# One-token attention over a KV cache: units of eight heads, V as the moving operand, q made transposed, wo loaded last

## The chip, the cores and the metric

The kernel runs on one core of one Trainium2 chip. The metric is the device time of one execution in microseconds (us); lower is better. The engines of the core are named as in the profile: PE is TensorE (PEld its weight loads), DVE is VectorE, ACT is ScalarE, POOL is GpSimd, SP is SyncE, which issues nearly all transfers (DMA) from HBM. Each engine works through its own instructions in program order and waits on semaphores for the others.

## The reference

Four sequences each decode one token. All arrays are bf16.

```python
B, Sq, D = 4, 1, 640;  H, Sk, Dh = 32, 4096, 128;  F = 1728
def _A_ref(x, k_cache, v_cache, wq, wo):
    q = (x @ wq).reshape(B, Sq, H, Dh).transpose(0, 2, 1, 3)
    scores = einsum("bhqd,bhkd->bhqk", q, k_cache) * (Dh ** -0.5)
    p = softmax(scores)
    o = einsum("bhqk,bhkd->bhqd", p, v_cache)
    return o.transpose(0, 2, 1, 3).reshape(B, Sq, H * Dh) @ wo
def _B_ref(x, w1, b1, w2):
    h = einsum("bsd,df->bsf", x, w1) + b1
    sp = log1p(exp(-abs(h))) + where(h > 0, h, 0)
    return einsum("bsf,fd->bsd", h * tanh(sp), w2)
h  = x + _A_ref(layernorm(x), k_cache, v_cache, wq, wo)
h2 = h + _B_ref(layernorm(h), w1, b1, w2)
```

K and V caches are 134 MB each and every element is used once; there is one query for each head and sequence.

## The kernel before

The schedule is manual: the order of the Python statements is the order of the instructions on each engine, and of the transfers on SP's queue. Tiles come from pools; a tile whose buffer is still in use makes its first writer wait, and where that writer is a transfer, everything behind it on SP's queue waits too.

The work is cut into 32 units g of four heads of one sequence. A K unit (L85, L89) is 4 MB: each head's 4096 positions are spread over 32 partitions, so that a partition holds R = 128 positions of 128 numbers, 32 KB. K and V have a pool of two buffers each; wq and later wo share a third (`wbig`).

For each unit, `mul_and_sum` (L288) multiplies K by q in place on DVE (L297), where q has been spread to all partitions (`qbs`), and sums over the 128 numbers of a position on PE: the identity is the stationary operand, K's columns move past it in eights of 64 positions (L304), and DVE adds the last eight (L316). A unit has two parts (`NP`) of two halves (`NQ`), so four multiplies, each followed by eight matmuls of 512 columns. `softmax` (L323) takes the maximum over a partition (L327), turns it into a row on PE (L329), takes the maximum for each head (L334), sends it back to all partitions (L342), and ACT makes the exps (L347) into `e2`, one instruction for each head on its 32 partitions, with the row sum on the side. `pv` (L225) multiplies by V with V as the stationary operand: 128 positions' rows of V are loaded as weights and a 128x4 piece of `e2` moves (L231), 128 times for a unit. After four units `row_sums` and `normalise` give `otn`, and `project` (L274) adds the heads' product with wo into `yT`.

The loop (L357) is a hand-made pipeline. The softmax of unit g-1 is a generator whose steps are put between the multiplies of unit g; after the multiplies of g come the load of K(g+2), pv(g-1), a projection, the load of V(g+1) and, in the first units, the next chunk of q (`q_chunk`, `q_broadcast`, L186 and L200). wo comes in four pieces at units 8 to 11, w1 and w2 at the end in K's freed buffer. Behind the loop are the last softmax, pv and projection, and then the dense part from `hT` (L440) to the output (L557).

Of the kernel before, what the change touches and what calls it, by code (L numbers as in the profile page):

```python
# [16 lines left out]
def kernel(  # L17
# [13 lines left out]

# [7 lines left out]
    G = 4  # L46
    PH = 128 // G
    R = Sk // PH
    NP = 2
    RP = R // NP  # L50
    W = 512 // RP
    HQ = H // G
    NG = HQ * N
    SCALE = float(Dh) ** -0.5
    EPS = 1e-5
    QC = 512
    WOC = 8
    NQ = 2
    DQ = Dh // NQ
    KBUFS = 2  # L60
    VBUFS = 2
    NE2 = 2

    CI = 4
# [7 lines left out]

    consts = ctx.enter_context(tc.tile_pool(name="consts", bufs=1))
    wbig = ctx.enter_context(tc.tile_pool(name="wbig", bufs=1))
    work = ctx.enter_context(tc.tile_pool(name="work", bufs=2))
    kpool = ctx.enter_context(tc.tile_pool(name="kpool", bufs=KBUFS))
    vpool = ctx.enter_context(tc.tile_pool(name="vpool", bufs=VBUFS))

    x_rows = A_x.rearrange("b s d -> (b s) d")
    out_rows = out.rearrange("b s (c p) -> (b s c) p", p=128)  # L80


    def load_kv(pool, tag, cache, g):
        hq, b = divmod(g, N)
        t = pool.tile([128, R, Dh], BF16, tag=tag, name=f"{tag}{g}")  # L85
        view = cache[b, G * hq : G * (hq + 1)].rearrange("h (p r) d -> (h p) r d", p=PH)

        np_ = NP if g == NG - 1 else 1
        for i in range(np_):  # L89
            r0, r1 = i * R // np_, (i + 1) * R // np_  # L90
            nc.sync.dma_start(out=t[:, r0:r1, :], in_=view[:, r0:r1, :])  # L91
        return t

    def load_k(g):
        return load_kv(kpool, "kt", A_k_cache, g)

    def load_v(g):
        return load_kv(vpool, "vt", A_v_cache, g)

    x_bf = consts.tile([N, D], BF16)  # L100
    nc.scalar.dma_start(out=x_bf[:, :], in_=x_rows[:, :])

    wq_sb = wbig.tile([128, DC, H * Dh], BF16, tag="w")
    nc.sync.dma_start(out=wq_sb[:, :, :], in_=A_wq.rearrange("(p c) n -> p c n", c=DC))
    kts, vts = {}, {}
    kts[0] = load_k(0)
    kts[1] = load_k(1)
    vts[0] = load_v(0)
# [8 lines left out]
    mean_f = consts.tile([128, 128], FP32)  # L117
    nc.gpsimd.memset(mean_f[:, :], 1.0 / D)
# [4 lines left out]
    sel = consts.tile([N, N, G, 128], BF16)  # L123
    nc.vector.memset(sel[:, :, :, :], 0.0)
    e2 = [consts.tile([128, R, G], BF16, name=f"e2_{i}") for i in range(NE2)]
    for t in e2:
        nc.gpsimd.memset(t[:, :, :], 0.0)
    rs2 = consts.tile([128, NG, G], FP32)
    nc.gpsimd.memset(rs2[:, :, :], 0.0)
    b1T = consts.tile([128, FC], FP32)  # L130
    nc.gpsimd.memset(b1T[:, :], 0.0)
    otn = consts.tile([128, HQ, N, G], BF16)

    for q in range(G):
        nc.vector.tensor_copy(
            out=sel[:, :, q, q * PH : (q + 1) * PH],
            in_=ident[0:N, 0:N].unsqueeze(2).to_broadcast([N, N, PH]),
        )

    def layernorm_rows(in_sb, out_bf, pool):  # L140
# [3 lines left out]
        for s in range(n_sub):  # L144
# [10 lines left out]
            out=out_bf[:, :],  # L155
            in0=in_sb[:, :],
# [6 lines left out]

# [3 lines left out]
    ln1_bf = consts.tile([N, D], BF16)  # L167
    layernorm_rows(x_bf, ln1_bf, work)
    xT = consts.tile([128, DC, N], BF16)
    xT_res = consts.tile([128, DC, N], FP32)  # L170
    ln1_v = ln1_bf[:, :].rearrange("n (p c) -> n c p", c=DC)
    x_v = x_bf[:, :].rearrange("n (c p) -> n c p", c=DC)
# [8 lines left out]
    q_all = consts.tile([N, H * Dh], BF16)  # L181

    def q_chunk(n):
        q_ps = ps.tile([N, QC], FP32, tag="qq")
        for c in range(DC):
            nc.tensor.matmul(  # L186
                q_ps[:, :],
                lhsT=xT[:, c, :],
                rhs=wq_sb[:, c, n * QC : (n + 1) * QC],
                start=(c == 0),  # L190
                stop=(c == DC - 1),
            )
        nc.scalar.copy(out=q_all[:, n * QC : (n + 1) * QC], in_=q_ps[:, :])  # L193

    def q_broadcast(hq):
        qb_ps = ps.tile([128, N * Dh], FP32, tag="qq")
        for b in range(N):
            for q in range(G):
                h = G * hq + q
                nc.tensor.matmul(  # L200
                    qb_ps[:, b * Dh : (b + 1) * Dh],
                    lhsT=sel[:, b, q, :],
                    rhs=q_all[:, h * Dh : (h + 1) * Dh],
                    start=(q == 0),
                    stop=(q == G - 1),
                )
        nc.scalar.copy(
            out=qbs[:, hq, :, :], in_=qb_ps[:, :].rearrange("p (b d) -> p b d", d=Dh)
        )

    qbs = consts.tile([128, HQ, N, Dh], BF16)

    Q_AT = {-1: (0,), **{g: (g + 1,) for g in range(HQ - 1)}}
    WO_AT = {HQ + i: i for i in range(H // WOC)}
    B1_AT = HQ + len(WO_AT) + 1

    PROJ_AT = {B1_AT + 1 + hq: hq for hq in range(4)}
    PROJ_AT.update({4 * (hq + 1) + 2: hq for hq in range(4, HQ - 1)})
    for hq in Q_AT[-1]:
        q_chunk(hq)  # L220
        q_broadcast(hq)

    ot = {}

    def pv(g):  # L225
        hq, b = divmod(g, N)
        vt = vts.pop(g)
        if b == 0:
            ot[hq] = ps.tile([128, N, G], FP32, tag="ot", bufs=2, name=f"ot{hq}")
        for r in range(R):  # L230
            nc.tensor.matmul(  # L231
                ot[hq][:, b, :],
                lhsT=vt[:, r, :],
                rhs=e2[g % NE2][:, r, :],
                start=(r == 0),
                stop=(r == R - 1),
            )

    rls = {}

    def row_sums(hq):
        l_ps = ps.tile([128, N, G], FP32, tag="small")
        nc.tensor.matmul(  # L243
            l_ps[:, :, :],
            lhsT=ones_f[:, :],
            rhs=rs2[:, hq * N : (hq + 1) * N, :],
            start=True,
            stop=True,
        )
        rls[hq] = work.tile([128, N, G], FP32, tag="rl", name=f"rl{hq}")  # L250
        nc.vector.reciprocal(out=rls[hq][:, :, :], in_=l_ps[:, :, :])  # L251

    def normalise(hq):
        nc.vector.tensor_tensor(
            out=otn[:, hq, :, :],
            in0=ot.pop(hq)[:, :, :],
            in1=rls.pop(hq)[:, :, :],
            op=ALU.mult,
        )

    b1_row = consts.tile([1, F], BF16)

    def f_chunk(rows, c):

        if c < CK * CI:
            k, i = divmod(c, CI)
            block = rows[:, k * 128 * CI : (k + 1) * 128 * CI]
            return block.rearrange("p (i f) -> p i f", i=CI)[:, i, :], 128
        return rows[:, c * 128 : min(F, (c + 1) * 128)], min(F - c * 128, 128)

    yT = ps.tile([128, DC, N], FP32, tag="yT")
    wo_sb = []

    def project(hq):  # L274

        for h in range(hq * G, (hq + 1) * G):
            for c in range(DC):
                nc.tensor.matmul(  # L278
                    yT[:, c, :],
                    lhsT=wo_sb[0][:, h, c * 128 : (c + 1) * 128],  # L280
                    rhs=otn[:, hq, :, h % G],
                    start=(h == 0 and c == 0),
                    stop=(h == H - 1 and c == DC - 1),
                )

    s_of, s_sbs = {}, {}

    def mul_and_sum(g, part):  # L288

        hq, b = divmod(g, N)  # L290
        r0 = part * RP
        kt = kts[g][:, r0 : r0 + RP, :]
        s_ps = ps.tile([128, RP, W], FP32, tag="s", bufs=2, name=f"s{g}_{part}")
        s_of[g, part] = s_ps
        for k in range(NQ):
            d0 = k * DQ
            nc.vector.tensor_tensor(  # L297
                out=kt[:, :, d0 : d0 + DQ],
                in0=kt[:, :, d0 : d0 + DQ],
                in1=qbs[:, hq, b, d0 : d0 + DQ].unsqueeze(1).to_broadcast([128, RP, DQ]),  # L300
                op=ALU.mult,
            )
            for d in range(d0, d0 + DQ, W):
                nc.tensor.matmul(  # L304
                    s_ps[:, :, :],
                    lhsT=ident[:, :],
                    rhs=kt[:, :, d : d + W],
                    start=(d == 0),
                    stop=(d == Dh - W),
                )  # L310
            yield

    def finish_sum(g, part):
        if part == 0:
            s_sbs[g] = work.tile([128, R], FP32, tag="s_sb", name=f"s_sb{g}")
        nc.vector.tensor_reduce(  # L316
            out=s_sbs[g][:, part * RP : (part + 1) * RP],
            in_=s_of.pop((g, part))[:, :, :],
            axis=AX.X,
            op=ALU.add,  # L320
        )

    def softmax(g):  # L323

        s_sb = s_sbs.pop(g)
        pm = work.tile([128, 1], FP32, tag="pm", name=f"pm{g}")
        nc.vector.tensor_reduce(out=pm[:, :], in_=s_sb[:, :], axis=AX.X, op=ALU.max)  # L327
        tr_ps = ps.tile([128, 128 + G], FP32, tag="tr", name=f"tr{g}")
# [99 lines left out]
    for _ in softmax(NG - 1):  # L428
        pass
# [159 lines left out]
```

## Time and profile before

| | |
|---|---|
| median of 3 runs | 678.37 us (678.27 to 678.69) |
| profiled execution | listed by its span: 676.7 us |
| moved by transfers | 284.15 MB, mean 420 GB/s |
| PE busy, PEld busy | 468.9 us (69%), 258.3 us (38%) |
| DVE busy | 353.1 us (52%) |
| ACT busy | 95.0 us (14%) |
| mean granted TensorE clock | 0.768 of full speed |

The span runs from the first to the last instruction; the rest of an execution's time lies around it. Busy times of different engines overlap, so they are not shares of one sum. A group line of the profile gives line, engine, operation, operands, count, busy time, mean nanoseconds of one, and behind the second bar the idle time of the engine just before and what ended most of it. PE's matmuls are pipelined: the duration of one is longer than the distance from one to the next.

### The profile page before, as it was taken

What the parts mean: (1) busy time and instruction counts of PE and PEld (TensorE: products, weight loads), DVE (VectorE), ACT (ScalarE), POOL (GpSimd) and SP (SyncE); (2) the same over time, 40 slices, a digit from 0 to 9 for tenths busy, and PEclk for the clock granted to TensorE, in tenths of its full rate; (3) what the DMA queues carried; (4) which work ended last, traced back from release to release, by engine and by line L of the source; (5) the groups of instructions that cost most, each with busy time, mean ns of one, the idle gap of its engine ahead of it and who ended that gap; (6) DMA issues with size and microseconds to landing.
All of it is one profiled execution on the core that took longest, in us unless ns stands there. A gap on an engine that the chain in (4) does not pass through costs nothing.

```text
span 676.7 us, 12413 instructions
## 1 busy us (share of the span) xinstructions
PE 468.9 (69%) x5761; PEld 258.3 (38%) x5761; DVE 353.1 (52%) x304; ACT 95.0 (14%) x313; POOL 2.4 (0%) x13
## 2 busy tenths in 40 slices
PE   1588988897676585476667767766766776666964
PEld 0234545444343341343334434333433433333444
DVE  2476555456654356336655545665554566555732
ACT  0022012112100111011100111110111111101131
POOL 1000000000000000000000000000000000000000
PEclk9997677887676786688667888766778877667875
DMA  9999999999999999999999999999999999999994
GB/s 378 434 429 431 433 430 430 432 431 432 426 427 422 429 415 411 431 422 431 427 427 426 431 431 431 431 433 431 430 429 429 427 433 429 433 430 425 431 394 165
DMA packets 16364, 284.15 MB, mean 420 GB/s; under 512 B 1268, under 2 KB 7096, under 8 KB 7737
## 3 DMA queue, kind: packets, MB, share of 16 engines
q1 hardware_dynamic: 16304, 283.36, 98.4%
q8 instruction: 45, 0.74, 0.4%
q14 instruction: 7, 0.05, 0.0%
q10 hardware_dynamic: 8, 0.01, 0.0%
HBM read 283.35 MB, written 0.01 MB: 419 GB/s over the span
## 4 chain that ended last, share of the span: by engine, by line
DMA 65%; PE 19%; DVE 14%; issue 1%; SPq 0%; ACT 0%; DVEq 0%
DMA kt<-in_A_k_cache_dram 61%; PE s L304 17%; DVE kt L297 12%; DMA w<-in_B_w_dram 4%; DVE s_sb L316 2%; PE tr L329 1%; PE ot L231 0%; PE h_ps L471 0%; PE y2T L533 0%; PE tr L342 0%; DVE mx L334 0%; SPq L91 0%; DVE tb L516 0%; ACT nbs L344 0%; PE var_ps L448 0%
## 5 line engine op out<-in xcount | busy, mean ns | idle before, releaser
L304 PE MATMUL s<-kt,ident 128*128 128x512 bf16 x1024 | 301.1, 448 | 171.9 <-DVE kt L297 171.5
L297 DVE TENSOR_TENSOR kt<-kt,qbs 128x4096 bf16<-128x4096 bf16 x128 | 291.5, 2279 | 217.9 <-DMA kt<-in_A_k_cache_dram 217.9
L304 PEld LDWEIGHTS <-ident 128*128 128x128 bf16 x1024 | 108.1, 109 | 324.7 <-issue 178.0
L231 PEld LDWEIGHTS <-vt 128*128 128x128 bf16 x4096 | 108.9, 96 | 11.3 <-DMA vt<-in_A_v_cache_dram 2.2
L231 PE MATMUL ot<-e,vt 128*128 128x4 bf16 x4096 | 108.9, 165 | 4.0 <-DMA vt<-in_A_v_cache_dram 2.1
L347 ACT ACTIVATE e<-s_sb,nbs 32x128 bf16<-32x128 f32 x128 | 74.0, 578 | 2.5
L344 ACT COPY nbs<-tr 128x4 f32<-128x4 f32 x32 | 5.2, 162 | 466.4 <-PE tr L342 466.4
L316 DVE TENSOR_REDUCE s_sb<-s 128x64 f32<-128x512 f32 x64 | 43.6, 681 | 4.4 <-PE s L304 4.2
L347 ACT ACTIVATION_READ_ACCUMULATOR e<-s_sb,nbs 32x1 f32 x128 | 32.2, 252 | 0.0
L251 DVE RECIPROCAL rl<-l_ps 128x16 f32<-128x16 f32 x8 | 2.1, 258 | 45.1 <-PE l_ps L243 45.1
L334 DVE TENSOR_REDUCE mx<-tr 1x4 f32<-1x128 f32 x32 | 8.9, 279 | 30.8 <-PE tr L329 30.8
L186 PE MATMUL q_ps<-wq_sb,xT 128*4 128x512 bf16 x40 | 15.0, 525 | 9.2 <-DMA wq_sb<-in_A_wq_dram 9.2
L200 PE MATMUL qb_ps<-q_all,sel 4*128 4x128 bf16 x128 | 14.1, 292 | 5.3 <-ACT q_all L193 5.3
L329 PE MATMUL tr<-ident_f,pm 128*1 128x128 f32 x64 | 16.3, 350 | 1.2 <-DVE pm L327 1.2
L200 PEld LDWEIGHTS <-sel 4*128 4x128 bf16 x128 | 12.8, 131 | 10.9 <-issue 10.9
L193 ACT CAST q_all<-q_ps 4x512 bf16<-4x512 f32 x8 | 4.6, 574 | 75.2 <-PE q_ps L186 75.2
L342 PEld LDWEIGHTS tr<-mx,nscale 1*128 1x128 f32 x64 | 9.4, 183 | 13.8 <-issue 11.4
L329 PEld LDWEIGHTS tr<-ident_f,pm 128*1 128x1 f32 x64 | 2.8, 81 | 26.0 <-issue 26.0
L342 PE MATMUL tr<-mx,nscale 1*128 1x4 f32 x64 | 12.2, 258 | 0.4 <-DVE mx L334 0.4
L327 DVE TENSOR_REDUCE pm<-s_sb 128x1 f32<-128x128 f32 x32 | 9.1, 286 | 1.1
L186 PEld LDWEIGHTS <-xT 128*4 128x4 bf16 x40 | 3.4, 98 | 15.1 <-issue 13.5
L278 PE MATMUL yT<-otn,wo_sb 128*128 128x4 bf16 x160 | 5.6, 166 | 2.8 <-issue 2.5
(74 smaller groups left out, 50.0 us busy)
## 6 DMA issues: line engine op xcount, KB each, us to landing
kt<-in_A_k_cache_dram SPq DMA_DIRECT2D x31, 4096.0 KB, 25.6
vt<-in_A_v_cache_dram SPq DMA_DIRECT2D x31, 4096.0 KB, 32.0
wq_sb<-in_A_wq_dram SPq DMA_DIRECT2D x1, 5120.0 KB, 14.8
wo_sb<-in_A_wo_dram SPq DMA_DIRECT2D x4, 1280.0 KB, 30.6
kt<-in_A_k_cache_dram SPq DMA_DIRECT2D x2, 2048.0 KB, 23.1
vt<-in_A_v_cache_dram SPq DMA_DIRECT2D x2, 2048.0 KB
w<-in_B_w_dram SPq DMA_DIRECT2D x1, 2160.0 KB, 27.8
w<-in_B_w_dram SPq DMA_DIRECT2D x3, 640.0 KB, 19.9
```

What stands on the lines that cost most here:

```text
L186: nc.tensor.matmul(q_ps[:, :], lhsT=xT[:, c, :], rhs=wq_sb[:, c, n * QC : (n + 1) * QC], start=(c == 0), stop=(c == DC - 1),)
L200: nc.tensor.matmul(qb_ps[:, b * Dh : (b + 1) * Dh], lhsT=sel[:, b, q, :], rhs=q_all[:, h * Dh : (h + 1) * Dh], start=(q == 0), stop=(q == ...
L231: nc.tensor.matmul(ot[hq][:, b, :], lhsT=vt[:, r, :], rhs=e2[g % NE2][:, r, :], start=(r == 0), stop=(r == R - 1),)
L278: nc.tensor.matmul(yT[:, c, :], lhsT=wo_sb[0][:, h, c * 128 : (c + 1) * 128], rhs=otn[:, hq, :, h % G], start=(h == 0 and c == 0), stop=(h ...
L297: nc.vector.tensor_tensor(out=kt[:, :, d0 : d0 + DQ], in0=kt[:, :, d0 : d0 + DQ], in1=qbs[:, hq, b, d0 : d0 + DQ].unsqueeze(1).to_broadcas ...
L304: nc.tensor.matmul(s_ps[:, :, :], lhsT=ident[:, :], rhs=kt[:, :, d : d + W], start=(d == 0), stop=(d == Dh - W),)
L316: nc.vector.tensor_reduce(out=s_sbs[g][:, part * RP : (part + 1) * RP], in_=s_of.pop((g, part))[:, :, :], axis=AX.X, op=ALU.add,)
L327: nc.vector.tensor_reduce(out=pm[:, :], in_=s_sb[:, :], axis=AX.X, op=ALU.max)
L329: nc.tensor.matmul(tr_ps[0:1, 0:128], lhsT=pm[:, :], rhs=ident_f[:, :], start=True, stop=True)
L334: nc.vector.tensor_reduce(out=mx[:, :], in_=tr_ps[0:1, 0:128].rearrange("o (a b) -> o a b", a=G), axis=AX.X, op=ALU.max,)
L342: nc.tensor.matmul(nb_ps, lhsT=nscale[:, :], rhs=mx[:, :], start=True, stop=True)
L347: nc.scalar.activation(out=e2[g % NE2][p0:p1, :, q], in_=s_sb[p0:p1, :], func=ACT.Exp, bias=nb[p0:p1, q : q + 1], scale=SCALE, accum_out=r ...
```

## The change

A unit u is now eight heads of one sequence (`G = 8`, 16 units), and a K or V unit is 64 KB to a partition (R = 256 positions on each of 16 partitions a head), 8 MB in one transfer. K, V, and the weights take turns in three slots of one pool: first wq (with x, its layernorm and b1 behind it in the same slot), then K(0), K(1), V(0), K(2), V(1), and so on, at the end wo with w1, and w2 with the small tiles of the dense part. The exps use all 128 partitions at a time: for head i the bias is the head's maximum on its own 16 partitions and -1e30 elsewhere (`own`), so that other heads' rows come out as zero. V is the moving operand: 32 columns of `e2` (eight heads by four positions) are the stationary one, and 512 columns of V move past them, 64 times a unit; the wanted diagonal of the 32 x 512 result is picked out by four fp32 matmuls with `sel`. q is made transposed, all heads at the start, wq as the stationary operand, and is spread to the partitions for each unit by an ACT copy (`qx`), a matmul with the identity and another ACT copy. The softmax is no longer cut into steps that stand between the multiplies of the next unit. wo is laid out with eight rows to a partition and is loaded behind the last V; the attention output is regrouped to that layout (`regroup`) and projected only behind the last unit. b1 is transposed at the start.

```diff
-    G = 4
+    G = 8
 ...
-    NP = 2
-    RP = R // NP
+    NO = H // G
+    NU = NO * N
+    RP = 64
+    NP = R // RP
 ...
+    slots = ctx.enter_context(tc.tile_pool(name="slots", bufs=3))
     consts = ctx.enter_context(tc.tile_pool(name="consts", bufs=1))
-    wbig = ctx.enter_context(tc.tile_pool(name="wbig", bufs=1))
     work = ctx.enter_context(tc.tile_pool(name="work", bufs=2))
-    kpool = ctx.enter_context(tc.tile_pool(name="kpool", bufs=KBUFS))
-    vpool = ctx.enter_context(tc.tile_pool(name="vpool", bufs=VBUFS))
+    one = ctx.enter_context(tc.tile_pool(name="one", bufs=1))
 ...
+    qT_ps = ps.tile([128, H, N], FP32, tag="qq", name="qT_ps")
+    for h in range(H):
+        for c in range(DC):
+            nc.tensor.matmul(
+                qT_ps[:, h, :],
+                lhsT=wq_sb[:, c, h * Dh : (h + 1) * Dh],
+                rhs=xT[:, c, :],
 ...
+    def q_broadcast(u):
+        o, b = divmod(u, N)
+        qx = one.tile([128, G, PH], BF16, tag="qx", name=f"qx{u}")
+        nc.scalar.copy(
+            out=qx[:, :, :],
+            in_=qT[:, G * o : G * (o + 1), b].unsqueeze(2).to_broadcast([128, G, PH]),
+        )
+        qb_ps = ps.tile([128, Dh], FP32, tag="qq", name=f"qb_ps{u}")
+        nc.tensor.matmul(
+            qb_ps[:, :],
+            lhsT=qx[:, :, :],
+            rhs=ident[:, :],
 ...
+        qbs[u] = work.tile([128, Dh], BF16, tag="qb", name=f"qb{u}")
+        nc.scalar.copy(out=qbs[u][:, :], in_=qb_ps[:, :])
 ...
+        for i in range(G):
             nc.scalar.activation(
-                out=e2[g % NE2][p0:p1, :, q],
-                in_=s_sb[p0:p1, :],
+                out=e2[:, :, i, :],
+                in_=s_sb[:, :].rearrange("p (g r) -> p g r", r=RQ),
                 func=ACT.Exp,
-                bias=nb[p0:p1, q : q + 1],
+                bias=nb[:, i : i + 1],
 ...
+    def pv(u):
+        o, b = divmod(u, N)
+        vt, e2 = vts.pop(u), e2s.pop(u)
+        l_ps = ps.tile([128, G], FP32, tag="small", name=f"l{u}")
+        nc.tensor.matmul(
+            l_ps[:, :], lhsT=ones_f[:, :], rhs=rss.pop(u)[:, :], start=True, stop=True
+        )
+        rl = one.tile([128, G], FP32, tag="rl", name=f"rl{u}")
+        nc.vector.reciprocal(out=rl[:, :], in_=l_ps[:, :])
+        o_ps = ps.tile([32, RQ * Dh], FP32, tag="o", name=f"o{u}")
+        for g in range(NGV):
+            nc.tensor.matmul(
+                o_ps[:, :],
+                lhsT=e2[:, g, :, :],
+                rhs=vt[:, g * RQ : (g + 1) * RQ, :],
 ...
+        o_sb = one.tile([32, RQ * Dh], FP32, tag="o_sb", name=f"o_sb{u}")
+        nc.scalar.copy(out=o_sb[:, :], in_=o_ps[:, :])
+        oT_ps = ps.tile([128, G], FP32, tag="oT", name=f"oT{u}")
+        for r in range(RQ):
+            nc.tensor.matmul(
+                oT_ps[:, :],
+                lhsT=o_sb[:, r * Dh : (r + 1) * Dh],
+                rhs=sel[:, r, :],
 ...
+        nc.vector.tensor_tensor(
+            out=otn[:, o, b, :], in0=oT_ps[:, :], in1=rl[:, :], op=ALU.mult
+        )
+
+    for u in range(NU):
+        scores(u)
+        if u + 2 < NU:
+            kts[u + 2] = load_kv("kt", A_k_cache, u + 2)
+        softmax(u)
+        if u + 1 < NU and u >= 1:
+            q_broadcast(u + 1)
+        if u >= 1:
+            pv(u - 1)
+        if u + 1 < NU:
+            vts[u + 1] = load_kv("vt", A_v_cache, u + 1, VQ if u + 1 == NU - 1 else 1)
 ...
+    pv(NU - 1)
 ...
+    for o in range(NO):
+        o8 = new_o8()
+        regroup(o, 0, N, o8)
+        project(o, o8)
```

`scores(u)` makes the same multiplies, matmuls and reduces as `mul_and_sum` and `finish_sum` did, in four parts of 64 positions, the reduce of one part behind the first half of the next, and the last reduce at its end. `regroup` makes one DVE multiply of `otn` with a mask (L400), four small matmuls (L407) and a DVE copy (L410); `project` makes 40 matmuls for its eight heads (L417). In the changed kernel the lines are: multiply L259, sum on PE L266, reduce L247, maximum L284, exps L304, qx L220, qb L225 and L233, row sum L318, V's product L325, o_sb L333, oT L336, otn L343. The dense part does the same operations in scratch tiles of the last slot.

## The prediction

> **What bounds the kernel now.** I read the page first (queues, chain), then the groups, then the timeline of a stretch in the middle and of the end. The first lines are the page's queue and the chain.
>
> ```profile
> q1 hardware_dynamic: 16304, 283.36, 98.4%
> DMA 65%; PE 19%; DVE 14%; issue 1%; SPq 0%; ACT 0%; DVEq 0%
> DMA kt<-in_A_k_cache_dram 61%; PE s L304 17%; DVE kt L297 12%; DMA w<-in_B_w_dram 4%; DVE s_sb L316 2%; PE tr L329 1%; PE ot L231 0%; PE h_ps L471 0%; PE y2T L533 0%; PE tr L342 0%; DVE mx L334 0%; SPq L91 0%; DVE tb L516 0%; ACT nbs L344 0%; PE var_ps L448 0%
> ```
>
> One queue keeps all 16 transfer engines busy for 98.4% of the span. PE and DVE are on the chain only because a K slot is free again when they are done. So the bound is bytes: a K or V of eight heads is 8.39 MB, and at about 431 GB/s it takes 19.4 us, a K and a V 38.9 us. All compute for eight heads has had 38.9 us of cover. The question is whether it still fits.
>
> The groups give the work that is under this cover:
>
> ```profile
> L304 PE MATMUL s<-kt,ident 128*128 128x512 bf16 x1024 | 301.1, 448 | 171.9 <-DVE kt L297 171.5
> L297 DVE TENSOR_TENSOR kt<-kt,qbs 128x4096 bf16<-128x4096 bf16 x128 | 291.5, 2279 | 217.9 <-DMA kt<-in_A_k_cache_dram 217.9
> L231 PE MATMUL ot<-e,vt 128*128 128x4 bf16 x4096 | 108.9, 165 | 4.0 <-DMA vt<-in_A_v_cache_dram 2.1
> ```
>
> The mean of a pipelined matmul hides its pitch, so I take that from the timeline. Columns: start, duration, engine, line, operation, idle before it and what ended that.
>
> ```profile
> 424.25 2.29 DVE L297 TENSOR_TENSOR kt<-kt,qbs 128x4096 bf16<-128x4096 bf16 x1 [8.05 <-DMA kt<-in_A_k_cache_dram]
> ...
> 426.60 3.57 PE L304 MATMUL s<-kt,ident 128*128 128x512 bf16 x8 [5.21 <-DVE kt L297]
> ...
> 433.25 1.89 PE L304 MATMUL s<-kt,ident 128*128 128x512 bf16 x8 [0.37 <-DVE kt L297]
> ...
> 437.78 3.37 PE L231 MATMUL ot<-e,vt 128*128 128x4 bf16 x128
> ...
> 453.08 0.58 ACT L347 ACTIVATE e<-s_sb,nbs 32x128 bf16<-32x128 f32 x1
> 453.41 0.25 ACT L347 ACTIVATION_READ_ACCUMULATOR e<-s_sb,nbs 32x1 f32 x1
> 453.67 0.59 ACT L347 ACTIVATE e<-s_sb,nbs 32x128 bf16<-32x128 f32 x1
> ```
>
> Eight matmuls of 512 columns take 1.89 us, with 0.38 for a single one a pitch of (1.89 - 0.38) / 7 = 0.216 us. After an idle 5.21 us the same eight take 3.57 (granted clock 0.50 in that stretch): 1.68 more. V's product for four heads is 3.37 us. Exps follow each other every 0.60 us; an exp's last 0.25 is the accumulator's read.
>
> The end shows the softmax chain without neighbours:
>
> ```profile
> 648.79 0.69 DVE L316 TENSOR_REDUCE s_sb<-s 128x64 f32<-128x512 f32 x1 [1.98 <-PE s L304]
> 649.51 0.29 DVE L327 TENSOR_REDUCE pm<-s_sb 128x1 f32<-128x128 f32 x1
> ...
> 651.30 0.58 ACT L347 ACTIVATE e<-s_sb,nbs 32x128 bf16<-32x128 f32 x1
> ```
>
> From the last reduce's start to the first exp: 2.51 us.
>
> **The change: order first.** Bytes stay the same. What changes is who waits. Before, softmax(g-1) and its exps stand between multiplies of unit g, and pv(g-1) fills PE while DVE waits for K. After, each engine works in program order through scores(u), softmax(u), q_broadcast(u+1), pv(u-1), and then scores(u+1):
>
> - ACT: qx(u+1) stands behind the eight exps of u. PE's qb matmul needs qx; behind it in PE's order are the row sum and all 64 matmuls of pv(u-1). So PE sits through the exps.
> - DVE: otn(u-1) (L343) stands ahead of the first multiply of u+1 (L259). It needs oT, which needs o_sb (ACT), which needs all of pv(u-1). So DVE sits through pv, and PE then waits for DVE's first multiply.
>
> Three engines take turns; the length of a unit is a sum, not a maximum.
>
> **The unit, term by term** (eight heads, one batch row):
> A. scores, first multiply to start of the last reduce. In the first unit's timeline three multiplies from 25.36 and a reduce that waits for slow-clock matmuls start the next step at 33.17: 7.81. A reduce and two multiplies then take 33.17 to 38.18 = 5.01, and there are two of these: 10.02. The third reduce and the last multiply are 0.61 + 2.27 = 2.88, the last eight matmuls and their handovers 1.98. Sum 22.7. The 1.1 us wait in the first part falls away if PE's clock is still up; a slower start as at 450.08 (2.46 for the second eight) adds 0.6.
> B. Last reduce to first exp: 2.51, with the maximum over 256 elements, not 128. L316 (512 elements, 681 ns) and L327 (128, 286 ns) give 1.03 ns an element: 2.64.
> C. Eight exps of 256 elements. L207 (512 elements, 585 ns) against L344 (4, 162 ns) gives 0.83 ns an element on ACT; 0.60 + 0.107 = 0.70, times 8 = 5.6. Bounds: nothing for the longer row (4.8), twice the price (9.6). I take the slope.
> D. qx (128 elements, about 0.3), qb's matmul and the row sum's two weight loads (0.50 at L243): 1.0.
> E. pv: 63 x 0.216 + 0.38 = 14.0, and 1.7 for the slow clock, as PE has had over 8 us with only tiny work: 15.7. Bounds 14.0 and 16.3. V was 2 x 3.37 = 6.7 us of PE for the same eight heads; it now moves 512 columns past 32 weights, and the nearest row for so narrow a stationary operand, L186 (4 columns; 5 matmuls in 1.24 us at 37.93), has the same pitch.
> F. o_sb (0.6), four fp32 matmuls (oT; L342 has 0.38 a pair, L243 0.58: 1.5 to 2.3, I take 1.5), otn 0.23: 2.4.
> T = 22.7 + 2.6 + 5.6 + 1.0 + 15.7 + 2.4 = 50.0 us, against 38.9 for its transfers.
>
> A rule of the Trainium skill speaks against term E (TensorE: Matmul & The Clock Gate, Part 3): with fewer than 128 columns in the stationary operand most of the array idles. This case's rows say how much: 14.0 us warm against 6.7 before. The sum above does not use it.
>
> **The transfers then have slack.** A slot comes free three loads later: K(u+2) takes V(u-1)'s slot, so it starts when pv(u-1) is done, lands some 20 to 22 us later and is wanted after a further 28 us. V(u+1) takes K(u+1)'s slot, starts as scores(u+1) end, is there some 22 us later, and pv(u+1) runs about 60 us after that start. SP's queue, in program order, holds no load that is due earlier. V(0) waits for wq's slot, which q's products release about 10 us after 15.6, long before K(1) has landed.
>
> **Around the units.** wq lands at 15.6 as before; K(0) of 8.39 MB needs two of the 9.7 us that 4.19 MB took (15.6 to 25.3): 35.0. qT (160 matmuls like L278's, 5.6 us, at half clock up to twice), b1 and the own, sel, dq_m and j_m masks lie under those 19.4 us: nothing, or up to 10 us if K(0) came at once. The removed q chunks and broadcasts (15.0 + 14.1 us of PE, 9.3 of ACT) were under transfers: nothing. Unit 0 has no pv: A + B = 25.3. Units 1 to 14: 14 x 50.0 = 700.
> Unit 15 has no qb, so pv(14) starts behind B while the exps run: 25.3 + 0.5 + 14.0 + 0.8 (half the slow start) + 2.4 = 43.0. pv(15) follows warm: 0.5 + 14.0 + 2.4, to 59.9. wo, w1 and w2 (9.6 MB, 22 us) wait for slots of K(15) and V(14), free after 22.7 and about 40 us of this unit. SP issues wo and w1 behind V(15), and w2 stands behind them; V(15) needs 20 us of the unit, wo and w1 17 more from 22.7, w2 5 more from 40 on. All are in by about 48.
> Then regroup and project for all four groups, none of it under anything: lm of 512 elements about 0.6; four times four small matmuls 0.3, a copy 0.25 and 40 matmuls 1.25 (20 took 0.67 at 663.01): 0.65 + 4 x 1.8 = 7.9. Before, only the last 20 were in the tail. From hT (663.73) to the end, 676.7, is 13.0, of which 1.6 was a wait for w1: 11.4.
> Span: 35.0 + 25.3 + 700 + 59.9 + 7.9 + 11.4 = 839.5. The page gives the profiled execution by its span alone, 676.7; the median of the runs is 1.7 above it. So 841 us.
> Ends of the terms: A -1.1 to +0.6, C -0.8 to +4.0, E -1.7 to +0.6, F 0 to +0.8 make T 46.4 to 56.0, the time 791 to 925 with all at one end.
>
> **Rivals.**
> 1. Slower still: the clock stays at half through pv. For it: the granted clock was 0.50 over 446.0 to 449.6, in a burst after 4.5 us of idle PE, and PE now idles longer each unit; no row has a long stream with 32 columns. Against: every 512-column stream of the trace is at 0.216 us within about 4 us, and the narrow L186 too. Price: a slow pitch of (3.57 - 0.6) / 7 = 0.42 makes pv 27.4, 11.7 more: 16 x 11.7 = 187, time 1028. Chance 0.07. The Trainium skill (same page, Part 1) has the gate open after one busy window of 3.4 us; by that this rival falls, and the trace's slow bursts agree, with their second eight at 1.95 to 2.46.
> 2. Not slower: transfers remain the bound, because pv(u-1) and the exps run beside scores(u). PE's sum would allow it: 14.0 + 14.0 and a few more of 38.9. It decides from T under 38.9, that is, if 11.1 us of C to F found cover. The bytes then end where they end now; the weights come last with wo first, so behind the last landing only y2T and the output remain: about 677. Against: the order on DVE and PE above, which gives no unit that overlap. Chance 0.03.
> 3. The change doesn't deliver long prefetch: a K that is late by its slot. At T = 50 its load has 28 us of slack; it would decide only below 38.9, where it is rival 2 with lost handovers of about 2 us a load (32 x 2 = 64): about 740. Chance 0.03.
>
> **Numbers.** My sum has 0.87: 841 us. The range leaves out rival 1, rivals 2 and 3 and the joint extremes: 797 to 900. A difference of 0.2% (1.4 us) is what a measurement here can tell; faster 0.02 and same 0.01 (both from rival 2), slower 0.97.
>
> **What would show it.** Right: queue share near 283.4 MB / 840 us (about 78 to 80%), chain with L259, L266, L325 and L304 and nearly no K transfer; units 50 us apart; 64 matmuls of L325 in 15 to 16 us, the first eight at 0.43; DVE's idle time before L343 (some 19 us a unit); exps 0.70 apart. Wrong: waits of L259 for kt's transfer, L325 at 0.43 throughout, or multiplies of u+1 that start before otn(u-1).

## The result and the profile after

The changed kernel takes 808.61 us (median of 4 runs, 807.48 to 810.75) where the kernel before took 678.37 (median of 4 runs too): a ratio of 1.192 (95% interval 1.1901 to 1.1938). The forecast was 841 us, with a range of 797 to 900. The profiled execution took 809.26 us, with a span of 807.4 and a mean granted TensorE clock of 0.897.

First the page after: the queue line (packets, MB, share of the 16 transfer engines' span) and the chain that ended last, by engine and by line.

```profile
q1 hardware_dynamic: 8254, 283.35, 83.7%
PE 51%; DVE 34%; ACT 9%; DMA 4%; issue 1%; SPq 0%; ACTq 0%; DVEq 0%
PE o L325 31%; DVE kt L259 27%; PE s L266 14%; ACT e L304 7%; DVE s_sb L247 5%; DMA kt<-in_A_k_cache_dram 4%; PE oT L336 2%; ACT o_sb L333 1%; DVE pm L284 1%; PE tr L297 1%; PE tr L286 1%; PE l L318 1%; PE yT L417 1%; DVE mx L290 1%; PE qb_ps L225 0%
```

The same bytes now occupy 83.7% of the span, not 98.4%, and K's transfers are 4% of the chain, not 61%. In their place stand four steps in a row: V's product on PE, the multiplies on DVE, the sums on PE, the exps on ACT. The chain passes from engine to engine, and the one percent of "issue" says that hardly any of it is unexplained.

The groups of the page after: line, engine, operation, operands, count, then busy time and mean ns of one, then the idle time of the engine ahead of it and what ended most of that.

```profile
L259 DVE TENSOR_TENSOR kt<-kt,qb 128x4096 bf16<-128x4096 bf16 x128 | 287.0, 2284 | 15.0 <-DMA kt<-in_A_k_cache_dram 15.0
L325 PE MATMUL o<-vt,e 128*32 128x512 bf16 x1024 | 248.7, 408 | 0.0
L343 DVE TENSOR_TENSOR otn<-oT,rl 128x8 bf16<-128x8 f32 x16 | 2.7, 167 | 272.5 <-PE oT L336 272.5
L304 ACT ACTIVATE e<-s_sb,nb 128x256 bf16<-128x256 f32 x128 | 63.1, 494 | 430.7 <-DVE nb L299 430.7
L225 PE MATMUL qb_ps<-ident,qx 128*128 128x128 bf16 x16 | 4.6, 288 | 64.0 <-ACT qx L220 63.9
```

DVE's multiplies waited 217.9 us for K before; now they wait 15.0, and that is the wait for the very first K. DVE's idle time has moved to L343, an instruction of 167 ns: 272.5 us, or 17.0 a unit, behind `oT`. PE sits 64.0 us ahead of `qb_ps`, for ACT's copy `qx`, which is ready only behind the eight exps.

One unit in the timeline after (start, duration, engine, line, operation, idle before it and what ended it):

```profile
253.05 6.70 DVE L259 TENSOR_TENSOR kt<-kt,qb 128x4096 bf16<-128x4096 bf16 x3
...
275.60 0.69 DVE L247 TENSOR_REDUCE s_sb<-s 128x64 f32<-128x512 f32 x1 [1.98 <-PE s L266]
...
278.27 0.51 ACT L304 ACTIVATE e<-s_sb,nb 128x256 bf16<-128x256 f32 x1 [26.47 <-DVE nb L299]
278.77 0.49 ACT L304 ACTIVATE e<-s_sb,nb 128x256 bf16<-128x256 f32 x1
...
282.21 0.28 ACT L220 COPY qx<-qT 128x128 bf16<-128x128 bf16 x1
282.55 0.29 PE L225 MATMUL qb_ps<-ident,qx 128*128 128x128 bf16 x1 [4.52 <-ACT qx L220]
...
283.10 15.79 PE L325 MATMUL o<-vt,e 128*32 128x512 bf16 x64
298.98 0.57 ACT L333 COPY o_sb<-o 32x512 f32<-32x512 f32 x1 [15.84 <-PE o L325]
299.61 1.05 PE L336 MATMUL oT<-sel,o_sb 32*128 32x8 f32 x8 [0.72 <-ACT o_sb L333]
300.70 0.17 DVE L343 TENSOR_TENSOR otn<-oT,rl 128x8 bf16<-128x8 f32 x1 [17.28 <-PE oT L336]
300.81 6.69 DVE L259 TENSOR_TENSOR kt<-kt,qb 128x4096 bf16<-128x4096 bf16 x3
```

Read the starts as a relay: last reduce, exps, `qx`, qb, V's product, its copy, its transposition, its scaling, and only then the first multiply of the next unit. This unit's own first multiply was at 253.05, so a unit is 47.76 us; the mean over units 1 to 14 (62.53 to 730.85) is 47.74.

### The profile page after: what moved, and what is told of

The parts are those of the page before. It is cut to its first block, busy times and chain, and to the rows that moved or that the text cites. A ratio compares the mean times of both kernels' runs of the same rounds, so it can differ in the third digit from the quotient of the medians.

```text
span 807.4 us, 6434 instructions
## 1 busy us (share of the span) xinstructions
PE 567.8 (70%) x2793; PEld 256.6 (32%) x2793; DVE 353.6 (44%) x314; ACT 87.8 (11%) x314; POOL 1.4 (0%) x10
## 3 DMA queue, kind: packets, MB, share of 16 engines
q1 hardware_dynamic: 8254, 283.35, 83.7%
HBM read 283.35 MB, written 0.01 MB: 351 GB/s over the span
## 4 chain that ended last, share of the span: by engine, by line
PE 51%; DVE 34%; ACT 9%; DMA 4%; issue 1%; SPq 0%; ACTq 0%; DVEq 0%
PE o L325 31%; DVE kt L259 27%; PE s L266 14%; ACT e L304 7%; DVE s_sb L247 5%; DMA kt<-in_A_k_cache_dram 4%; PE oT L336 2%; ACT o_sb L333 1%; DVE pm L284 1%; PE tr L297 1%; PE tr L286 1%; PE l L318 1%; PE yT L417 1%; DVE mx L290 1%; PE qb_ps L225 0%
## 5 line engine op out<-in xcount | busy, mean ns | idle before, releaser
L266 PE MATMUL s<-kt,ident 128*128 128x512 bf16 x1024 | 264.5, 412 | 113.2 <-DVE kt L259 113.2
L259 DVE TENSOR_TENSOR kt<-kt,qb 128x4096 bf16<-128x4096 bf16 x128 | 287.0, 2284 | 15.0 <-DMA kt<-in_A_k_cache_dram 15.0
L325 PE MATMUL o<-vt,e 128*32 128x512 bf16 x1024 | 248.7, 408 | 0.0
L266 PEld LDWEIGHTS <-ident 128*128 128x128 bf16 x1024 | 106.5, 104 | 264.9 <-issue 159.1
L325 PEld LDWEIGHTS <-e 128*32 128x32 bf16 x1024 | 104.2, 103 | 136.9 <-issue 33.2
L343 DVE TENSOR_TENSOR otn<-oT,rl 128x8 bf16<-128x8 f32 x16 | 2.7, 167 | 272.5 <-PE oT L336 272.5
L304 ACT ACTIVATE e<-s_sb,nb 128x256 bf16<-128x256 f32 x128 | 63.1, 494 | 430.7 <-DVE nb L299 430.7
L247 DVE TENSOR_REDUCE s_sb<-s 128x64 f32<-128x512 f32 x64 | 44.0, 687 | 48.7 <-PE s L266 47.6
L225 PE MATMUL qb_ps<-ident,qx 128*128 128x128 bf16 x16 | 4.6, 288 | 64.0 <-ACT qx L220 63.9
L333 ACT COPY o_sb<-o 32x512 f32<-32x512 f32 x16 | 9.2, 575 | 246.8 <-PE o L325 246.8
L336 PE MATMUL oT<-sel,o_sb 32*128 32x8 f32 x128 | 16.9, 254 | 11.5 <-ACT o_sb L333 11.5
L304 ACT ACTIVATION_READ_ACCUMULATOR e<-s_sb,nb 128x1 f32 x128 | 23.8, 186 | 0.0
L225 PEld LDWEIGHTS <-qx 128*128 128x128 bf16 x16 | 1.7, 104 | 65.5 <-ACT qx L220 65.5
L336 PEld LDWEIGHTS oT<-sel,o_sb 32*128 32x128 f32 x128 | 15.4, 186 | 19.4 <-ACT o_sb L333 19.4
L286 PE MATMUL tr<-ident_f,pm 128*1 128x128 f32 x32 | 6.1, 270 | 21.3 <-DVE pm L284 21.3
L318 PE MATMUL l<-rs,ones_f 128*128 128x8 f32 x32 | 8.4, 335 | 0.0
```

The lines of the kernel that those rows point to most:

```text
L247: nc.vector.tensor_reduce(out=s_sbs[u][:, part * RP : (part + 1) * RP], in_=s_ps[:, :, :], axis=AX.X, op=ALU.add,)
L259: nc.vector.tensor_tensor(out=kt[:, :, d0 : d0 + DQ], in0=kt[:, :, d0 : d0 + DQ], in1=qbs[u][:, d0 : d0 + DQ].unsqueeze(1).to_broadcast([1 ...
L266: nc.tensor.matmul(s_ps[:, :, :], lhsT=ident[:, :], rhs=kt[:, :, d : d + W], start=(d == 0), stop=(d == Dh - W),)
L286: nc.tensor.matmul(tr_ps[0:1, 0:128], lhsT=pm[:, :], rhs=ident_f[:, :], start=True, stop=True)
L304: nc.scalar.activation(out=e2[:, :, i, :], in_=s_sb[:, :].rearrange("p (g r) -> p g r", r=RQ), func=ACT.Exp, bias=nb[:, i : i + 1], scale= ...
L318: nc.tensor.matmul(l_ps[:, :], lhsT=ones_f[:, :], rhs=rss.pop(u)[:, :], start=True, stop=True)
```

## Experiments

The theory: the length of a unit is a sum because program order puts two handovers into it. **Wait 1**: PE's qb stands behind ACT's exps, and V's product stands behind qb. **Wait 2**: DVE's `otn` stands behind V's product, and the next multiplies stand behind `otn`. The rivals: V's product by itself is the cost, whatever the order; or the 8 MB units and three slots bring K too late. All ratios are to the kernel before, with 95% intervals.

### Wait 1 taken away: q spread ahead of the scores

```diff
     for u in range(NU):
+        if u + 1 < NU and u >= 1:
+            q_broadcast(u + 1)
         scores(u)
 ...
         softmax(u)
-        if u + 1 < NU and u >= 1:
-            q_broadcast(u + 1)
```

> The changed kernel with q_broadcast(u+1) at the head of iteration u, so that PE's qb matmul no longer stands behind the eight exps of u and ahead of pv(u-1). Theory (a unit is a sum of turns): from the last reduce to pv's first matmul 2.7 us, as in unit 15 of the changed kernel, not 7.5; pv starts with the clock up, 14.0 and not 15.8; unit 47.75 - 4.8 - 1.8 = 41.1, time 808.6 - 14 x 6.6 = 716 (705 to 735). Rival (three slots and 8 MB loads make the time, the order does not matter): 800 to 810.

Measured: 731.54 us, 1.0777 (1.0761 to 1.0793), 77 us less than the changed kernel. Timeline of this kernel:

```profile
298.89 0.51 ACT L304 ACTIVATE e<-s_sb,nb 128x256 bf16<-128x256 f32 x1 [24.97 <-DVE nb L299]
298.90 13.99 PE L325 MATMUL o<-vt,e 128*32 128x512 bf16 x64
```

V's product of the unit before now starts together with the first exp and is 13.99 us long, not 15.79: the exps are hidden, and PE starts at full speed, without the idle of 4.52 us that stood ahead of its work in the changed kernel (granted clock 1.00 over 298.90 to 302.50). A unit with such a start is 22.6 + 2.7 + 14.0 + 1.8 = 41.1 us. The gain fell short of the expected 716, within its range, since every few units PE started slow all the same and took up to 1.8 us more (units of 41.2 to 43.0). The product at 172.84 is such a one: 15.67 us, granted clock 0.65 over its first 3.7 us, though the idle times just ahead of it are the same as at 298.90. So idle time alone doesn't decide the clock; what does is not shown. A change of place alone, with the same instructions, is worth 77 of the 130 us lost, so V's product by itself isn't the whole cost.

### Wait 2 taken away: the end of V's product behind the next unit's first reduce

```diff
+                    if part == 1 and late:
+                        finish(*late.pop())   # reciprocal, o_sb, oT, otn of pv(u - 1)
 ...
-            pv(u - 1)
+            late.append(pv(u - 1))
```

> The changed kernel with the end of pv(u-1) (reciprocal, o_sb, oT, otn) behind the first reduce of scores(u+1); the qb matmul stays behind the exps. Theory: DVE makes the first three multiplies of u+1 while PE does pv, the first reduce comes 3.6 us after pv's last matmul and not 9.6; unit about 47.75 - 5.7 = 42.0, time 808.6 - 14 x 5.7 = 729 (718 to 745). Rival (slots and 8 MB loads): 800 to 810.

Measured: 774.84 us, 1.1422 (1.1403 to 1.1441): 34 us gained, much less than expected, and outside the range given (718 to 745). Timeline of this kernel:

```profile
317.46 16.64 PE L326 MATMUL o<-vt,e 128*32 128x512 bf16 x64
...
337.70 0.69 DVE L248 TENSOR_REDUCE s_sb<-s 128x64 f32<-128x512 f32 x1 [13.47 <-PE s L267]
...
339.32 1.05 PE L343 MATMUL oT<-sel,o_sb 32*128 32x8 f32 x8
340.41 0.17 DVE L350 TENSOR_TENSOR otn<-oT,rl 128x8 bf16<-128x8 f32 x1 [1.91 <-PE oT L343]
...
345.96 0.69 DVE L248 TENSOR_REDUCE s_sb<-s 128x64 f32<-128x512 f32 x1 [0.99 <-PE s L267]
```

The first half of the mechanism is there: the first reduce of the next unit starts 337.70 - 334.10 = 3.6 us behind V's product, since its multiplies ran beside it. But the edit has a wait of its own: `otn` now stands right behind that reduce on DVE, and `oT` stands behind 24 matmuls on PE, so DVE waits 1.91 us there and the second reduce comes at 345.96, 8.26 behind the first where two multiplies and a reduce need 5.0. About 3 us a unit are given back. V's product, slow at its start, takes 16.64 here.

### Both edits

The edits of the last two diffs together:

```diff
+            q_broadcast(u + 1)                # ahead of scores(u)
+                        finish(*late.pop())   # behind the first reduce
```

> Both order edits together, V still the moving operand. Theory: compute for a unit falls to about 35.5 us (2.7 + 14.0 + 3.6 + 15.2), under the 38.9 of its transfers; the transfers bind again, units 38.9 apart, time about 677 (665 to 690). Rival (V as the moving operand costs more than the cover holds, 28 us of PE for a unit plus its handovers): 41 us a unit or more, over 710.

Measured: 701.35 us, 1.0339 (1.0318 to 1.0361). The gains nearly add (77 + 34 = 111; 107 measured). This lies between the expected range (665 to 690) and the rival's (over 710): neither was right. In the timeline, what is left is the wait that the second edit added and an end at which two products of V, each of 15.67 us, follow each other on PE with nothing beside them.

### The second edit without its own wait

The end of V's product is cut in two: `o_sb` and `oT` behind the first reduce of the next unit, the reciprocal and `otn` behind the third, by when `oT` has long been done. q is spread ahead, as before.

```diff
+                    if part == 1 and late:
+                        late.append(turn(*late.pop()))     # o_sb, oT
+                    if part == 3 and late:
+                        normalise(*late.pop())             # reciprocal, otn
```

> As e3_both, V the moving operand, but o_sb and oT stay behind the first reduce of scores(u+1) and the reciprocal and otn come behind the third, so that DVE does not wait for oT (3 us a unit in e2 and e3). Theory: compute 2.7 + 14.0 + 3.6 + 15.2 = 35.5 a unit, transfers bind at 38.9 to 39.2, V(15) lands by 640 and the last pv ends by 655: 676 (668 to 688). Rival (V moving cannot be covered): 697 or more, as e3.

Measured: 680.55 us (678.1 to 682.74), 1.0027 (1.0014 to 1.0039). It is 4.5 us above the expectation of 676, of which some 2 lie at its end (below), and far from the rival's 697. Its waits (engine and tile, releaser, us in total, times, longest):

```profile
DVE kt L260 <- DMA kt<-in_A_k_cache_dram: 182.0, 14, 15.5
```

DVE waits for K again, in 14 places (the first K among them), up to 15.5 us each, and the queue is busy for 97.5% of the span: the transfers set the pace. Not all of this wait is to spare, as PE makes V's product during most of it. Early on, two products start 37.24 us apart (162.82 and 200.06), with K there at 171.81, before the first of them ends; so compute sets that distance, and it has some 1.7 us to spare under 38.9. V is still the moving operand here, with all of its 14.0 to 15.7 us a unit; the 130 us lost are gone down to 2. So the order was the cause: V's product costs time only where it stands in the sum.

### V as the stationary operand, everything else as in the change

256 matmuls with V's rows as weights and eight columns of `e2`, laid out `[128, R, G]` as in the kernel before; no `o_sb`, and `oT` comes out directly. The order stays.

```diff
-        e2 = work.tile([128, NGV, G, RQ], BF16, ...)
+        e2 = work.tile([128, R, G], BF16, ...)
 ...
+        for r in range(R):
+                oT_ps[:, :], lhsT=vt[:, r, :], rhs=e2[:, r, :],
```

> The changed kernel with its own order, but V as the stationary operand (256 weight loads of 128x128 with 8 columns of e2, e2 laid out position by head; no o_sb and oT). Theory (sum of turns): pv 256 x 0.0264 = 6.8 us and otn 0.4 in place of 15.8 + 1.9; unit 37.3 to 38.2, just under the 38.9 of transfers; time about 675 (664 to 695). Rival (taking turns is the loss whatever V's operand): 45 us a unit, 765 or more. Exps: 0.49 apart if 128 partitions made them cheaper than before; 0.7 if what made them dear before was writing 2-byte elements with a stride.

Measured: 772.03 us, 1.138 (1.134 to 1.1419), against an expected 675. That is the rival's number (765 or more). PE's own work is short as reckoned, but two other times appear. Timeline of this kernel:

```profile
228.51 1.60 ACT L304 ACTIVATE e<-s_sb,nb 128x256 bf16<-128x256 f32 x1
229.64 1.60 ACT L304 ACTIVATE e<-s_sb,nb 128x256 bf16<-128x256 f32 x1
...
246.08 1.79 PE L325 MATMUL oT<-e,vt 128*128 128x8 bf16 x61 [3.19 <-issue]
```

The exps follow each other every 1.13 us instead of 0.49: each stores 256 elements of two bytes, 16 bytes apart. Eight of them take 8.89 us in this unit (227.55 to 236.44), and with wait 1 still in place PE sits through all of it. And V's 256 matmuls have a gap of 3.19 us, for which the profile names no releaser. So this run doesn't tell the theory from its rival; the same with rows of `e2` in one piece tells more:

```diff
-        e2 = work.tile([128, R, G], BF16, ...)
+        e2 = work.tile([128, G, R], BF16, ...)
 ...
+                rhs=e2[:, :, r],
```

> As e4_v_stationary, but e2 laid out head by position, so that an exp writes 256 elements in a row and the matmul's moving 8 columns are 512 bytes apart. In e4 the exps were 1.13 us apart (0.49 in the changed kernel) and PE had a gap of 3.2 us in each 256 matmuls that nothing shown releases. Theory (the store's stride makes the exps dear): 0.49 or less apart; unit 45.4 - 5.1 = 40.3, time 772 - 14 x 5.1 = 700 (690 to 712). Rival (128 weight loads wide pv slows ACT, or exps are dear for another reason): 1.1 apart, 765 to 775. The gap in pv stays if it hangs on the number of PE instructions, and goes if it hung on the exps.

Measured: 700.98 us, 1.0317 (1.0302 to 1.0332), as expected; the layout alone is worth 71 us. Timeline:

```profile
251.92 0.49 ACT L304 ACTIVATE e<-s_sb,nb 128x256 bf16<-128x256 f32 x1
252.41 0.49 ACT L304 ACTIVATE e<-s_sb,nb 128x256 bf16<-128x256 f32 x1
```

The exps are at 0.49 again. The gap in V's product stays (2.88 us in this unit), so it doesn't hang on the exps. Halving PE's work on V gives back 808.6 - 701.0 = 108 of the 130 us, where both changes of order gave 128: either shortens the sum to near what the transfers need.

### V stationary and q spread ahead

`e2` in rows with V stationary, as in the run of 700.98 us, and the edit of the first experiment:

```diff
+            q_broadcast(u + 1)   # ahead of scores(u)
```

> e4b with q_broadcast(u+1) at the head of iteration u. Theory: unit of compute 22.5 + 2.7 + 10.3 + 0.3 = 35.8, under the 38.9 of its transfers: the transfers bind, DVE waits for K again, time 668 (660 to 682), equal to the kernel before or below it. Rival (8 MB loads in three slots cannot keep the queue full): 690 or more with the queue's share under 95%.

Measured: 676.45 us, 0.997 (0.9958 to 0.9982): 0.3% under the kernel before, the only version with a gain besides the one below. It is in the expected range, but 8 us above the 668 that was reckoned. Queue line of its page:

```profile
q1 hardware_dynamic: 8254, 283.35, 97.9%
```

The transfers set the pace again, and the rival (a share under 95%) falls. The chain of its last 45 us holds five waits of PE without a releaser, 1.94, 1.98, 2.62, 1.12 and 1.24 us, 8.9 in all; the next experiment looks at them.

### Its end in another order

The first three groups' masks are made ahead of V's last product, and their regrouping and projection fill PE while the last `otn` is made; the same edit on the kernel in two steps, with V moving.

```diff
+    for o in range(NO - 1):
+        mask(o)
+    last = pv(NU - 1)
+    gather(0, o8s[0])
+    gather(1, o8s[1])
+    normalise(*last)
+    mask(NO - 1)
+    project(0, o8s[0])
 ...
```

> e5b with the end rearranged: the masks of three head groups are made ahead of the last pv, and their regrouping and projection run on PE while the last otn and mask are made. In e5b the last otn to hT took 10.2 us; here about 6.5. Theory: 673 (670 to 676), below the kernel before. Rival (the last weights to land, not this chain, set the end): 676 to 677, as e5b.

> e3b (V the moving operand) with the same rearranged end. In e3b the last pv ended at 655.0 and hT began at 664.4, 9.3 us; here about 7. Theory: 678 (675 to 680). Rival (the end hangs on the landing of the last weights): 680 to 681, as e3b.

Measured: 676.75 us, 0.9972 (0.9961 to 0.9982), with V stationary: nothing gained on 676.45. With V moving: 678.1 us, 0.9992 (0.9984 to 1.0001), no difference from the kernel before; without the edit the ratio was 1.0027. PE at the end, V stationary, old end:

```profile
649.70 2.33 PE L325 MATMUL oT<-e,vt 128*128 128x8 bf16 x81 [2.62 <-issue]
...
655.90 0.19 PE L396 MATMUL o<-j_m,wend 128*128 128x8 bf16 x1 [1.12 <-issue]
...
662.09 0.18 PE L406 MATMUL yT<-wend,wend 128*128 128x4 bf16 x1 [1.24 <-issue]
```

and with the new end:

```profile
649.68 2.33 PE L323 MATMUL oT<-e,vt 128*128 128x8 bf16 x81 [2.62 <-issue]
...
655.88 0.19 PE L417 MATMUL yT<-wend,wend 128*128 128x4 bf16 x1 [2.16 <-issue]
...
662.08 0.19 PE L417 MATMUL yT<-wend,wend 128*128 128x4 bf16 x1 [2.16 <-issue]
```

PE resumes behind its gaps at the same instants, every 6.2 us, whatever work stands there. The new end has more work done ahead of the gaps, and the two behind V's product grow from 1.12 and 1.24 us to 2.16 each: that is where its gain went. The time is the one that the rival gave, but not for its reason: behind 605 us the chain holds no transfer, and no instruction waits for the weights' landing.

### More transfer on purpose

The changed kernel, with the first 1 MB of each V of units 1 to 14 loaded a second time ahead of the whole.

```diff
+        if kind == "vt" and 1 <= u < NU - 1:
+            nc.sync.dma_start(out=tv[:, 0:32, :], in_=view[:, 0:32, :])
```

> The changed kernel with 1 MB of each V (units 1 to 14) loaded twice: the first piece, a wait for its landing, then the whole V, so about 2.4 us of transfer and 2 of waiting more for each unit (38.9 to about 43.4). Theory (the unit is 47.75 us of turns and its transfers have 8.9 us of slack): 808 to 814. Rival (the 8 MB transfers through three slots set the time): 14 x 4.4 = 62 more, 870.

Measured: 808.69 us, 1.192 (1.1904 to 1.1937), against 808.61 without. Queue line of its page:

```profile
q1 hardware_dynamic: 10270, 298.03, 87.6%
```

14.7 MB more, none of it in the time. The transfers of the changed kernel have slack, so the three slots and the 8 MB loads don't set its time; the rival of a late K falls.

### The exps' layout in the kernel before

```diff
-    e2 = [consts.tile([128, R, G], BF16, ...
+    e2 = [consts.tile([128, G, R], BF16, ...
 ...
-                out=e2[g % NE2][p0:p1, :, q],
+                out=e2[g % NE2][p0:p1, q, :],
```

> The kernel before with e2 laid out head by position (exps of 128 elements on 32 partitions write rows without a stride). If the store's stride made its exps dear (0.60 apart for 128 elements, against 0.49 for 256 in the changed kernel, which writes four in a row): 0.35 to 0.42 apart. If 32 partitions instead of 128 made them dear: 0.58 to 0.60. The time stays at 678 (677 to 680) either way, as ACT is under the transfers.

Measured: 678.83 us, 1.0002 (0.9993 to 1.0011). The exps' line in this kernel (ns of one: least, median, most; first and last start):

```profile
L347 ACT ACTIVATE e<-s_sb,nbs x128: 395/399/402, 47.5 to 653.6; 32x128 bf16<-32x128 f32 x128
```

399 ns where the kernel before has 578, and 0.50 us from one exp to the next where it had 0.60. This is between the two expectations (0.35 to 0.42 and 0.58 to 0.60 apart). So the stride of the store (8 bytes in the kernel before) was part of its price, and 0.08 us or more of the spacing is not explained. The time doesn't move, as ACT lies under the transfers there.

## Why the prediction was right, and where it was off

**Order first: right.** It named the two handovers, and the experiments that take them away bring the transfers back as the bound. DVE's idle time ahead of L343 is 17.0 us a unit (19 had been said), and there is no multiply of the next unit ahead of `otn`.

**The unit, term by term**, for the unit from 253.05 to 300.81:

| term | said | measured, from the timeline | |
|---|---|---|---|
| A scores | 22.7 | 22.55 | 253.05 to 275.60 |
| B to the first exp | 2.6 | 2.67 | to 278.27 |
| C eight exps | 5.6 | 3.94 | to 282.21 |
| D qx, qb | 1.0 | 0.89 | to 283.10 |
| E V's product | 15.7 | 15.88 | to 298.98 |
| F copy, oT, otn | 2.4 | 1.83 | to 300.81 |
| T | 50.0 | 47.76 | |

**The size: 32 us too much, in two terms.** Fourteen units at 47.74, not 50.0, are 668.3 instead of 700: 31.7 us, nearly the whole miss. Mostly it is C, 1.66 a unit, and below the lower bound that I gave it (4.8). I put a slope for the longer row on top of the 0.60 us that an exp of 128 elements took in the trace of before; an exp of 256 elements is at 0.49. The 0.60 was not an exp's price without its store: with rows in one piece the same exp is at 0.50, so 0.10 of the 0.60 belonged to a layout that the change removes. That 256 elements on 128 partitions then follow each other no slower than 128 elements on 32 partitions is measured (0.49 and 0.50) and not explained. The rest is F, 0.57: the four fp32 products of `oT` take 1.05 us, below the 1.5 to 2.3 taken from single pairs: the trace has eight matmuls of 254 ns each there, which overlap.

**Around the units** the errors cancel. K(0)'s first multiply is at 36.26 (35.0 said); unit 0 takes 26.27 (25.3; a wait of 2.17 at its first reduce, for slow-clock matmuls); unit 15 takes 57.1 (59.9; both of its V products run at full speed, 13.99 us, where 0.8 had been added to the first, and what follows each of them is shorter than said), regroup and project 7.5 (7.9), the rest 12.0 (11.4).

**The transfers: right in kind.** They have slack, as the doubled loads show. The queue's share is 83.7%, not 78 to 80: the span is shorter, and the queue was busy for 0.837 x 807.4 = 676 us for the same bytes, where the kernel before needed 0.984 x 676.7 = 666.

**The rivals.** Half clock through all of pv (1028 us) falls: E's 15.79 us is 1.80 above the 13.99 of the warm one, in which 64 matmuls are at (13.99 - 0.38) / 63 = 0.216 us. The granted clock is 0.52 over 283.10 to 286.90 and 1.00 from there to 298.90, so the slow stretch is about 3.8 us. The Trainium skill (TensorE: Matmul & The Clock Gate, Part 1) opens the gate after about 3.4 us of sustained work; the trace agrees, and for 32-column weights too. The transfers as the bound (677) and a K late by its slot (740) didn't come; the first of them is what the kernels with another order reach.

## What to carry to other kernels

Where each engine works in program order, a short producer (here a copy and a matmul that spread q) goes ahead of a long consumer's inputs, and a step that needs another engine's long result goes behind the next unit's work, at a place where that result is already there: the same instructions then took 681 us rather than 809 (678 with the end rearranged too). Before giving a product's operands other roles, count the busy time that each choice gives the engine, and ask whether it has cover; and price a store's layout on the producer's side too, as one transposed layout of the exps cost 71 us where PE waited for them, and nothing measurable in the kernel before, where they lie under transfers.

## What the runs showed of the hardware

- **Stores of ACT.** Exps of 256 elements follow each other every 0.49 us when they store rows or runs of four elements, and every 1.13 us when each two-byte element lies 16 bytes from the next. Exps of 128 elements on 32 partitions are 0.60 us apart with elements 8 bytes from each other and 0.50 in rows.
- **Gaps of PE without a releaser.** With V stationary, PE stops for up to 4.2 us within the 256 matmuls of a unit, and at the end of the kernel it resumes every 6.2 us. The waits of the run of 676.45 us, and a row of the kernel before:

```profile
PE oT L325 <- issue: 49.8, 18, 4.2
...
656.04 0.46 PE L231 MATMUL ot<-e,vt 128*128 128x4 bf16 x12 [1.88 <-issue]
```

Between two resumptions at the end lie 128 matmuls with their 128 weight loads, 256 instructions. The queue that the page calls instruction moves 45 packets of 0.74 MB in all there, 16 KB each, against 22 with V moving, where no such gap is over 0.3 us. The kernel before moves 45 packets too, but runs 128 of V's matmuls at a time; it shows one such gap within V's product, the second row above, at its end, where two products follow each other. That PE waits for its next instructions fits, but no run tested it by itself, so it stays open.
- **Larger loads.** The queue's busy time is 0.979 x 674.2 = 660 us for 283.35 MB in the fastest version, against 666 us before: 429 GB/s against 426. In the changed kernel, with the same 8 MB loads, it is 676 us, 419 GB/s. So the runs don't show that loads of 8 MB instead of 4 MB are worth anything by themselves; one percent is the most that they show.
